# Second chunk's queries loaded in 128-byte pieces and turned on VectorE, and another order of the first stages

## The chip, the cores and the metric

The kernel runs on one core of one Trainium2 chip. The metric is the time of one execution on the device in microseconds; before the change the median of three runs is 737.36 us (735.57 to 737.45).

## The reference

Pooled attention is followed by a gated feed-forward layer. Keys and values are averaged over groups of eight positions (576 become 72), each head's queries attend to the averaged keys, and the result of all heads is the input `x` of 4608 tokens by 512.

```
k_p = k.reshape(B, H, Sp, pool, D).mean(axis=3)          # B = H = 8, S = 576, D = 64, pool = 8
v_p = v.reshape(B, H, Sp, pool, D).mean(axis=3)
scores = scale * np.matmul(q, k_p.transpose(0, 1, 3, 2))
attn = softmax(scores)
x = np.matmul(attn, v_p) as [tokens, heads * D]          # 4608 x 512
a = x @ w1
b = x @ w2
out = (a * b @ w3) @ w_out                               # w1, w2: 512 x 1024; w3: 1024 x 1024; w_out: 1024 x 512
```

## The kernel before

The product `w3 @ w_out` does not depend on the tokens, so it is made first, once, as `W` (1024 x 512); after it each token needs `a`, `b`, their product and one product with `W`. Products run in a 32-bit format with fewer bits, so each operand is split into a high and a low part, and three products (high-high, high-low, low-high) stand for one.

The weights are 64-bit numbers, loaded raw as pairs of 32-bit words and turned into 32-bit numbers on the chip: `w_high` on ScalarE (L144) and `w_low` on VectorE or ScalarE (L149, L154, by the list `LOW_ACT`) make two halves, `w_or` on VectorE (L158) joins them. For `w3` TensorE turns the result (`w_turn`, L187) and `t_hi` (ScalarE, L192) and `t_lo` (VectorE, L195) split it; for `w_out` `o_hi` (L199) and `o_lo` (L203, VectorE or GpSimd by `O_POOL`) do. `w_mm` (L633) multiplies, into the four banks `o0`, `o1`, `o2` and `a` and then `b`; `w_hi` and `w_lo` (L640, L644) split `W`. `w1` and `w2` go the same way without a turn (`load_w12` L135, `w12_high`, `w12_low`, `w12_or`, `w12_hi` L237, `w12_lo` L242 on VectorE or GpSimd by `LO_DVE`). `warm` (L211) is four transposes that nothing reads.

The tokens are worked in 12 chunks of 384. For chunk `m`, `a_mm m j` and `b_mm m j` (L556, twelve products of 128x384 each, j from 0 to 7) fill banks `a` and `b`; `a_post` (L566, ScalarE, or VectorE where `A_DVE` says so) empties `a`, `g_mul` (L574) multiplies, `g_hi` and `g_lo` (L579, L585) split, and `out_mm` (L601) multiplies with `W`. The attention of chunk `n` is done among the products of chunk `n - 1`: keys are averaged by `prep_k` (a tree of three additions on GpSimd, L380 to L385, or a reduction on VectorE, L340, by `K_DVE`), turned by `kt_mm` (L354) and copied by `kt_post`; `s_mm` (L432) makes the scores, `soft_*` on VectorE and ScalarE the softmax, `pt_mm` or `pt_turn` turn it, `av_mm` (L529) multiplies with the averaged values, and `x_hi` and `x_lo` split the result. From the third chunk on one of the score banks is bank `a`.

Queries must be turned before `s_mm`. There are two ways. `load_q3` (L290) loads tokens onto partitions in pieces of 256 bytes, `q3_turn` (L299) turns them on TensorE, three transposes for each of the four pairs of heads, and `q3_post` (L305) copies them out on ScalarE or VectorE (`Q_DVE`). `load_q` (L270) loads blocks of 32 tokens by 32 numbers, 128 bytes at a time, so that `tr_q` (L281), one 32x32 block transpose on VectorE for each pair, puts them in place. `Q3N` lists the chunks that go the first way. The second chunk lies in two batches, so `load_q3` issues two DMAs for a pair of heads and `load_q` eight.

Each step is a function that records its instructions, and `ORDER` names all steps up to the fourth chunk in the order in which they are recorded; the rest follows by due times. Every engine, and SyncE's queue of DMAs, runs its instructions in that order, and semaphores hold it where something it needs is not there.

Of the kernel before, what the change touches and what calls it, by code (L numbers as in the profile page):

```python
# [19 lines left out]
def kernel(  # L20
# [790 lines left out]
    for b in range(1, B):  # L811
# [17 lines left out]
        warm 5; warm 6; w_mm 0 2 (1,); load_w3 4; w_mm 0 3 (0,); t_lo 0; w_mm 1 0 (2,); o_hi 3; o_lo 3;
        w_high w3 3; w_mm 0 2 (0,); w_mm 1 1 (2,); load_wo 2; w_low w3 5; w_low w3 3; w_turn 2; t_hi 2;  # L830
        w_or w3 3; w_mm 0 3 (1,); t_lo 2; w_mm 0 1 (0,); w_mm 0 1 (2,); w_high w3 5; w_mm 1 3 (2,);
        w_mm 1 2 (0,); load_wo 7; w_or w3 5; load_wo 5; w_low w3 4; w_high wo 4; w_low wo 4; w_or wo 4;
        w_mm 1 3 (1,); w_high w3 4; w_or w3 4; w_high wo 2; w_low wo 2; w_or wo 2; w_mm 1 1 (0,); w_mm 1 2 (2,);
        load_w3 6; w_mm 0 1 (1,); w_mm 2 1 (0,1,2); w_mm 0 3 (2,); load_w3 8; w_turn 3; t_hi 3; t_lo 3;
        w_low wo 5; w_low wo 7; w_mm 2 3 (0,1,2); load_wo 6; w_mm 0 2 (2,); w_mm 0 0 (2,); warm 10; w_turn 5;
        w_turn 4; o_hi 2; load_w3 7; w_mm 1 1 (1,); o_lo 2; w_high wo 7; t_hi 4; t_lo 4; w_mm 1 3 (0,);
        w_high wo 5; w_mm 3 1 (0,1,2); o_hi 4; w_high w3 6; w_mm 3 3 (0,1,2); w_or wo 5; w_mm 3 0 (0,1,2);
        load_q3 0 0; w_low w3 6; o_hi 5; w_or w3 6; o_lo 4; w_mm 2 0 (0,1,2); load_w3 10; w_low wo 6; o_lo 5;
        w_low w3 8; w_mm 3 2 (0,1,2); w_mm 4 0 (0,1,2); w_mm 4 2 (0,1,2); t_hi 5; w_high wo 6; t_lo 5;
        w_high w3 7; w_or wo 7; w_low w3 7; w_mm 2 2 (0,1,2); load_k 0 0; load_k 0 1; w_turn 6; t_hi 6;  # L840
        w_mm 4 3 (0,1,2); w_high w3 8; load_q3 0 3; w_or w3 7; w_mm 5 1 (0,1,2); w_mm 5 3 (0,1,2); warm 3;
        w_mm 5 0 (0,1,2); o_hi 7; q3_turn 0 0; q3_post 0 0; w_low w3 10; w_or wo 6; load_w3 9; load_k 0 2;
        o_hi 6; w_turn 7; t_hi 7; w_or w3 8; w_mm 4 1 (0,1,2); t_lo 6; w_mm 5 2 (0,1,2); o_lo 7; o_lo 6;
        load_q3 0 2; w_turn 8; w_mm 6 1 (0,1,2); t_lo 7; w_mm 7 1 (0,1,2); prep_k 0 0; w_mm 6 0 (0,1,2);
        load_w3 11; w_hi 0 0; w_lo 0 0; w_mm 7 3 (0,1,2); w_mm 7 2 (0,1,2); w_high w3 10; w_mm 6 3 (0,1,2);
        q3_turn 0 3; q3_post 0 3; load_q3 0 1; prep_k 0 1; w_low w3 9; load_w3 13; t_hi 8; w_high w3 9; t_lo 8;
        w_or w3 10; prep_k 0 2; w_mm 7 0 (0,1,2); w_mm 6 2 (0,1,2); load_v 0 0; prep_v 0 0; kt_mm 0; w_hi 0 2;
        kt_post 0; load_w3 12; w_mm 8 0 (0,1,2); w_turn 10; w_lo 0 2; w_low w3 11; q3_turn 0 2; t_hi 10;
        w_or w3 9; w_hi 0 1; w_mm 8 3 (0,1,2); q3_post 0 2; t_lo 10; w_lo 0 1; w_high w3 11; w_mm 8 1 (0,1,2);
        load_w3 15; q3_turn 0 1; w_or w3 11; w_turn 9; w_mm 10 3 (0,1,2); warm 11; w_turn 11; w_low w3 13;  # L850
        t_hi 9; t_lo 9; w_mm 8 2 (0,1,2); w_mm 9 1 (0,1,2); warm 1; q3_post 0 1; s_mm 0 (0,); soft_max 0 0 0 0;
        t_hi 11; t_lo 11; w_high w3 13; load_w3 14; load_v 0 1; w_low w3 12; w_hi 0 3; w_mm 9 3 (0,1,2);
        w_mm 9 2 (0,1,2); soft_max 0 0 1 0; w_mm 10 0 (0,1,2); w_mm 9 0 (0,1,2); s_mm 0 (1,); w_mm 10 1 (0,1,2);
        w_high w3 12; w_or w3 13; soft_exp 0 0 0; w_low w3 14; prep_v 0 1; load_w12 0 1; w_mm 10 2 (0,1,2);
        w_or w3 12; w_high w3 14; w_or w3 14; w_turn 14; soft_max 0 1 0 0; soft_max 0 1 1 0; soft_sub 0 1 0 0;
        w_mm 11 1 (0,1,2); soft_sub 0 1 1 0; w_lo 0 3; soft_exp 0 0 1; soft2 0 0; t_hi 14; w_turn 12; w_turn 13;
        load_v 0 2; soft_exp 0 1 0; t_hi 12; t_lo 12; w_mm 11 3 (0,1,2); t_hi 13; w_mm 11 0 (0,1,2); t_lo 14;
        pt_mm 0 0 4 6; w_mm 11 2 (0,1,2); soft_exp 0 1 1; soft_sum 0 1 0; soft_sum 0 1 1; w12_high 0 1; t_lo 13;
        load_w12 0 0; w12_high 0 0; pt_mm 0 0 0 4; w_mm 12 3 (0,1,2); pt_post 0 0 4 6; load_w12 1 1; soft2 0 1;
        load_q3 1 0; w_high w3 15; pt_post 0 0 0 4; s_mm 0 (2,); soft_max 0 2 0 0; w_mm 14 0 (0,1,2);  # L860
        load_q3 1 3; w12_low 0 0; w_mm 12 0 (0,1,2); soft_max 0 2 1 0; pt_mm 0 1 4 6; w12_low 0 1; w12_or 0 0;
        pt_post 0 1 4 6; soft_exp 0 2 0; w12_low 1 1; soft_exp 0 2 1; w_mm 14 1 (0,1,2); w_low w3 15;
        w_or w3 15; pt_mm 0 1 0 4; w_mm 13 3 (0,1,2); w12_high 1 1; w12_or 0 1; w_mm 13 1 (0,1,2); w_turn 15;
        prep_v 0 2; w_mm 14 3 (0,1,2); w_mm 14 2 (0,1,2); w12_hi 0 0; w12_or 1 1; soft2 0 2; load_w12 2 0;
        w12_hi 1 1; q3_turn 1 0; w_mm 12 1 (0,1,2); pt_mm 0 2 4 6; pt_post 0 1 0 4; load_q3 1 1; t_hi 15;
        t_lo 15; w12_low 2 0; w12_lo 0 0; move_v 0 0; load_w12 1 0; w12_low 1 0; w12_high 1 0; w12_or 1 0;
        load_w12 2 1; w12_hi 0 1; w_hi 1 0; pt_mm 0 2 0 4; pt_post 0 2 4 6; pt_post 0 2 0 4; q3_turn 1 1;
        w_mm 15 3 (0,1,2); q3_post 1 0; w_mm 15 1 (0,1,2); q3_post 1 1; w12_low 2 1; w12_lo 1 1; w12_high 2 0;
# [108 lines left out]
```

## Time and profile before

| | |
|---|---|
| runs | 735.57, 737.36, 737.45 us; median 737.36 |
| profiled execution | 736.2 us, its span 734.4 us |
| TensorE busy | 719.3 us (98%) |
| VectorE, ScalarE, GpSimd busy | 404.6, 226.8, 188.2 us |
| mean granted TensorE clock | 0.999 |
| chain that ended last | TensorE 91%, DMA 3%, VectorE 2%, ScalarE 2% |

The span runs from the first to the last instruction of the profiled execution, and 1.8 us of its time lie around it. Busy time of TensorE counts each matmul from its start to its modelled end, and since matmuls overlap, a share of 98% doesn't say that nothing is lost. What is lost is read from its waits and from how far apart its instructions start.

### The profile page before, as it was taken

The numbers are of one execution on the slowest core, as the hardware profiler recorded it, in microseconds if no ns is written. First come the engines' busy times: TensorE is split into PE (matmuls) and PEld (weight loads), VectorE is DVE, ScalarE is ACT, GpSimd is POOL, SyncE is SP. The second block draws the span as 40 slices with busy tenths as digits, with TensorE's granted clock in tenths as the row PEclk, the third lists the DMA queues.
The fourth block names the chain that finished last, engine by engine and source line by source line (L and its number), as shares of the span: only waits on it lengthen the run. The fifth ranks groups of instructions, "written<-read, shape, count | busy, mean of one in ns | idle before, by whom it ended". The sixth has DMA issues, their size and how long they took to land.

```text
span 734.4 us, 13643 instructions
## 1 busy us (share of the span) xinstructions
PE 719.3 (98%) x5450; PEld 650.3 (89%) x5450; DVE 404.6 (55%) x789; ACT 226.8 (31%) x503; POOL 188.2 (26%) x243
## 2 busy tenths in 40 slices
...
GB/s 335 302 252 270 268 165 105 106 109 84 70 58 17 143 65 2 81 127 83 75 113 93 95 65 3 91 124 73 98 100 91 89 65 2 86 24 1 43 1 44
DMA packets 117391, 73.78 MB, mean 100 GB/s; under 512 B 76496, under 2 KB 94416, under 8 KB 117328
## 3 DMA queue, kind: packets, MB, share of 16 engines
...
q10 hardware_dynamic: 144, 0.13, 0.1%
...
## 4 chain that ended last, share of the span: by engine, by line
PE 91%; DMA 3%; DVE 2%; ACT 2%; SPq 1%; issue 1%; POOL 0%; DVEq 0%
PE a L556 27%; PE b L556 27%; PE o L601 26%; PE o L633 3%; PE a L529 3%; PE att L432 2%; DMA st<-in_k_dram 1%; PE a L432 1%; PE b L633 1%; DMA raw<-in_moe_w_dram 1%; PE att L529 1%; PE att L187 1%; DMA PT<-T 1%; PE att L354 0%; DVE EB L449 0%
## 5 line engine op out<-in xcount | busy, mean ns | idle before, releaser
L556 PE MATMUL a<-xT,hl 128*128 128x384 f32 x1152 | 217.4, 336 | 0.2 <-ACT a L566 0.2
L556 PE MATMUL b<-xT,hl 128*128 128x384 f32 x1152 | 216.7, 336 | 0.3 <-DVE a L574 0.3
L556 PEld LDWEIGHTS a<-xT,hl 128*128 128x128 f32 x1152 | 203.4, 188 | 7.7 <-ACT a L566 1.0
L556 PEld LDWEIGHTS b<-xT,hl 128*128 128x128 f32 x1152 | 200.9, 188 | 2.1 <-DVE a L574 0.6
L601 PE MATMUL o<-Wc,gh 128*128 128x512 f32 (+1 forms) x576 | 180.3, 394 | 0.0
L574 DVE TENSOR_TENSOR a<-b,a 128x384 f32<-128x384 f32 x96 | 52.9, 551 | 195.4 <-PE b L556 192.9
L380 POOL TENSOR_TENSOR st<-st 96x512 f32<-96x512 f32 (+3 forms) x52 | 69.5, 1336 | 294.1 <-DMA st<-in_k_dram 207.0
L601 PEld LDWEIGHTS o<-Wc,gh 128*128 128x128 f32 x576 | 105.9, 188 | 22.6 <-issue 4.7
L601 PE MATMUL o<-Wc,gl 128*128 128x512 f32 (+1 forms) x288 | 113.3, 393 | 0.0
L579 ACT CAST gh<-a 128x384 fp32r<-128x384 f32 x96 | 49.3, 513 | 189.7 <-DVE a L574 188.4
L566 ACT COPY a<-a 128x384 f32<-128x384 f32 x91 | 43.6, 479 | 172.7 <-PE a L556 157.0
L585 DVE TENSOR_TENSOR gl<-a,gh 128x384 fp32r<-128x384 f32 x96 | 58.7, 611 | 32.1 <-ACT gh L579 32.1
L601 PEld LDWEIGHTS o<-Wc,gl 128*128 128x128 f32 x288 | 54.1, 188 | 12.5 <-DVE gl L585 0.3
L457 ACT ACTIVATE EB<-EB 128x288 f32<-128x288 f32 x66 | 29.0, 444 | 88.5 <-DVE EB L449 88.5
L508 DVE STREAM_TRANSPOSE T<-EB 128x768 f32<-128x768 f32 x33 | 51.4, 1558 | 6.3 <-DMA PT<-T 6.1
L469 DVE TENSOR_REDUCE sm<-EB 128x4 f32<-128x288 f32 x66 | 29.5, 449 | 28.7 <-ACT EB L457 28.7
L633 PE MATMUL o<-hl 128*128 128x512 f32 x144 | 42.1, 421 | 0.0
L381 POOL TENSOR_TENSOR st<-st 96x256 f32<-96x256 f32 (+3 forms) x52 | 39.8, 766 | 4.1
L398 POOL DMA_DIRECT2D vm<-vp x64 | 32.2, 511 | 2.1 <-POOL vp L385 2.0
L633 PEld LDWEIGHTS o<-hl 128*128 128x128 f32 x144 | 26.7, 197 | 5.9 <-ACT hl L192 0.7
L444 DVE TENSOR_REDUCE mx<-att 128x4 f32<-128x288 f32 (+2 forms) x72 | 28.0, 397 | 3.9 <-PE att L432 3.8
L476 DVE TENSOR_TENSOR EB<-EB,sm 128x576 f32<-128x576 f32 x36 | 28.6, 793 | 1.2
...
## 6 DMA issues: line engine op xcount, KB each, us to landing
...
```

The costliest lines, as they stand in the source:

```text
L380: nc.gpsimd.tensor_tensor(out=t[:, :, 0:4], in0=t[:, :, 0:4], in1=t[:, :, 4:8], op=ALU.add)
L381: nc.gpsimd.tensor_tensor(out=t[:, :, 0:2], in0=t[:, :, 0:2], in1=t[:, :, 2:4], op=ALU.add)
L398: nc.gpsimd.dma_start(out=vm[b % 2][32 * g:32 * g + KW, c], in_=vp[b][KW * i:KW * i + KW, s])
L469: nc.vector.tensor_reduce(out=Mt[n, t][1][:, hs], in_=parts(Et[n, t])[:, hs], axis=AX.XY, op=ALU.add)
L508: nc.vector.transpose(out=T.rearrange("p g u i -> p u g i"), in_=Et[n, t][:, :NU * P].rearrange("p (u j g) -> p u g j", u=NU, g=4))
L556: nc.tensor.matmul(out=o, lhsT=w12[j - j % 2 + kt // 2, w][sw][:, c:c + P], rhs=x[sx][:, kt], start=(i == 0), stop=(i == 3 * NK - 1))
L566: (nc.vector.tensor_copy if (m, j) in A_DVE else nc.scalar.copy)(out=a, in_=stage.pop(("a", m, j))[:, :CH])
L574: nc.vector.tensor_tensor(out=g, in0=ps[:, :CH], in1=g, op=ALU.mult)
L579: nc.scalar.copy(out=gh, in_=g)
L585: nc.vector.tensor_tensor(out=gl, in0=g, in1=f(gh), op=ALU.subtract)
L601: nc.tensor.matmul(out=oacc[m][t][x][:, cols], lhsT=(gh, gl)[sg][:, c], rhs=W[j][sw][:, cols], start=(k == 1 and i == 0), stop=(k == NJ an ...
L633: nc.tensor.matmul(out=wacc[h][it], lhsT=w3t[s][sa][:, x * P:(x + 1) * P], rhs=wo[j][sb], start=n == 1, stop=n == 3 * NJ)
```

## The change

The second chunk is taken out of `Q3N`, so its queries come by `load_q` and are turned by `tr_q`: 12 transposes on TensorE and four copies go, 32 DMAs of 24 KB stand for eight of 96 KB, and VectorE gets four block transposes. Lists that choose an engine change with it: all `a_post` go to ScalarE, some steps of the weights change engine, and the first batch's keys go from VectorE to GpSimd. `ORDER` is another one up to the fourth chunk; after that the steps follow as before.

```
-    LO_DVE = [(0, 0), (1, 0), (1, 1), (2, 0), (7, 0), (7, 1)]
+    LO_DVE = [(1, 1), (2, 0), (2, 1), (3, 1), (4, 0), (4, 1), (6, 0), (6, 1), (7, 1)]
...
-        ('w3', 0), ('w3', 1), ('w3', 10), ('w3', 11), ('w3', 2), ('w3', 3), ('w3', 9), ('wo', 0),
-        ('wo', 4), ('wo', 6)]
-    LOW_DVE = [(0, 1), (1, 1), (2, 1), (5, 0), (7, 1)]
-    O_POOL = [2, 4, 6]
-    A_DVE = [(0, 0), (0, 1), (0, 2), (0, 5), (0, 6)]
-    Q_DVE = [(0, 2), (0, 3), (1, 0), (1, 1), (1, 3)]
-    PT_DVE = [(0, 1, 0), (0, 1, 4), (0, 2, 4), (1, 0, 4), (1, 1, 4), (1, 2, 4)]
+        ('w3', 0), ('w3', 10), ('w3', 13), ('w3', 14), ('w3', 15), ('w3', 2), ('w3', 4), ('w3', 9),
+        ('wo', 2), ('wo', 3), ('wo', 4), ('wo', 7)]
+    LOW_DVE = [(1, 0), (1, 1), (2, 1), (3, 1), (5, 1), (6, 1)]
+    O_POOL = [0, 4, 7]
+    A_DVE = []
+    Q_DVE = [(0, 3)]
+    PT_DVE = [(0, 0, 4), (0, 1, 0), (0, 1, 4), (1, 0, 4), (1, 1, 4), (1, 2, 4)]
     COLD = [0, 1, 10, 11, 2, 3, 4, 6, 7, 8, 9]
-    Q3N = (0, 1)
+    Q3N = (0,)
     PTN = (0,)
-    K_DVE = [(0, 0), (1, 2), (1, 3)]
+    K_DVE = [(1, 3)]
...
-        warm 4; load_wo 0; warm 8; w_high wo 0; warm 7; load_w3 1; w_high w3 1; w_low w3 1; w_low wo 0;
+        load_w3 0; w_low w3 0; w_high w3 0; load_w3 1; w_high w3 1; w_low w3 1; w_or w3 1; w_or w3 0; warm 5;
...
-        a_post 2 5; move_v 2 1; move_v 2 0; av_mm 3; b_mm 2 5; g_hi 2 4; x_hi 3 0; x_hi 3 3; a_mm 2 6; g_lo 2 4;
-        x_lo 3 0; x_lo 3 3; tr_q 4 1; x_hi 3 2; x_lo 3 2; x_hi 3 1; tr_q 4 2; s_mm 4 (0,1,2); g_mul 2 5;
+        a_mm 2 6; x_lo 3 1; b_mm 2 5; g_mul 2 5; s_mm 4 (0,1,2); soft_max 4 1 0 0; soft_sub 4 1 0 0;
```

The first four loads were `wo 0`, `w3 1`, `w3 0`, `w3 2` and are now `w3 0`, `w3 1`, `wo 0`, `w3 2`. Behind `s_mm 4` the two orders differ too: before, `out_mm 2 3`, `out_mm 2 4` and `b_mm 2 6` stand between it and `a_mm 2 7`, which fills bank `a` again; now `out_mm 2 4` alone does. Of the numbers of `warm` only 5 does something.

The first place is TensorE's start. `att<-ident,Wc` are the turns of `w3`, `o<-hl` and `a<-hl` the first products of the weights, and `att<-ident` is `warm`. Before:

```order
L187 MATMUL att<-ident,Wc 128x128 x8
L633 MATMUL o_136<-hl 128x512
L633 MATMUL a<-hl 128x512
L633 MATMUL o_134<-hl 128x512 x2
L633 MATMUL o_136<-hl 128x512
L211 MATMUL att<-ident 128x128 x4
L633 MATMUL o_135<-hl 128x512 x2
```

On the same engine, after the change:

```order
L211 MATMUL att<-ident 128x128 x4
L187 MATMUL att<-ident,Wc 128x128 x8
L633 MATMUL o_154<-hl 128x512
L633 MATMUL a<-hl 128x512
L187 MATMUL att<-ident,Wc 128x128 x4
L633 MATMUL o_154<-hl 128x512
L633 MATMUL o_156<-hl 128x512 x2
```

The warming transposes moved ahead of everything, and a third turn stands after two products.

The second place is ScalarE's start, which makes the first operands: L144 and L154 make the halves of the weights (`Wc` for `w3`, `wt` for `w_out`), L192 is `t_hi`, L199 `o_hi`. Before:

```order
L144 ACTIVATE wt<-raw 128x512
L144 ACTIVATE Wc<-raw 128x512
L154 ACTIVATE Wc<-raw 128x512
L154 ACTIVATE wt<-raw 128x512
L154 ACTIVATE Wc<-raw 128x512
L144 ACTIVATE Wc<-raw 128x512
L199 CAST hl<-wt 128x512
L192 CAST hl<-att 128x512
```

On ScalarE after the change:

```order
L154 ACTIVATE Wc<-raw 128x512
L144 ACTIVATE Wc<-raw 128x512 x2
L144 ACTIVATE wt<-raw 128x512
L144 ACTIVATE Wc<-raw 128x512
L154 ACTIVATE Wc<-raw 128x512
L192 CAST hl<-att 128x512
L199 CAST hl<-wt 128x512
L192 CAST hl<-att 128x512
```

Six operations on weights, the last two on the fourth load (`w3 2`), now stand ahead of the first two splits, where before six stood there too, on three loads.

The third place is SyncE's queue around the second chunk's queries (`qs`); `raw` are loads of `w1` and `w2` there, `st` those of keys and values. Before, from two loads of `w1` and `w2` on:

```order
L135 DMA raw<-in_moe_w_dram 128x2x512 x2
L290 DMA qs<-in_q_dram 64x6x64 x4
L135 DMA raw<-in_moe_w_dram 128x2x512
L290 DMA qs<-in_q_dram 64x6x64 x2
L135 DMA raw<-in_moe_w_dram 128x2x512 x3
L326 DMA st<-in_k_dram 64x512
L326 DMA st<-in_k_dram 128x2x512 x2
L290 DMA qs<-in_q_dram 64x6x64 x2
L135 DMA raw<-in_moe_w_dram 128x2x512 x3
```

On SyncE after the change:

```order
L135 DMA raw<-in_moe_w_dram 128x2x512 x2
L326 DMA st<-in_k_dram 128x2x512
L270 DMA qs<-in_q_dram 32x6x32 x8
L135 DMA raw<-in_moe_w_dram 128x2x512 x3
L270 DMA qs<-in_q_dram 32x6x32 x8
L326 DMA st<-in_k_dram 128x2x512
L135 DMA raw<-in_moe_w_dram 128x2x512
L270 DMA qs<-in_q_dram 32x6x32 x8
L135 DMA raw<-in_moe_w_dram 128x2x512
L326 DMA st<-in_k_dram 64x512
L270 DMA qs<-in_q_dram 32x6x32 x8
```

The loads of queries come in four groups of eight, between loads of weights and keys, where one group of four and two of two stood.

On GpSimd the trees of the first batch's keys were those of the second and third part; now it makes all three, first, third and second, and `kt_mm 0` on TensorE, which needs them, stands behind 105 products of the weights instead of 96.

## Rows read from the trace of the kernel before

**Rows 1.** busy time, share and instructions of each engine, page part 1

```profile
PE 719.3 (98%) x5450; PEld 650.3 (89%) x5450; DVE 404.6 (55%) x789; ACT 226.8 (31%) x503; POOL 188.2 (26%) x243
```

**Rows 2.** TensorE's waits: line and releaser, total us, times, longest

```profile
PE att L187 <- DVE Wc L158: 9.1, 2, 8.6
PE att L354 <- POOL km L385: 0.8, 1, 0.8
PE a L432 <- ACT a L566: 0.6, 1, 0.6
PE b L556 <- DVE a L574: 0.3, 1, 0.3
```

**Rows 3.** TensorE's timeline, first 25 us: start, us, instructions, idle before

```profile
8.64 1.09 PE L187 MATMUL att<-ident,Wc 128*128 128x128 f32 x4 [8.64 <-DVE Wc L158]
...
11.00 0.78 PE L633 MATMUL o<-hl 128*128 128x512 f32 x1
...
13.57 1.06 PE L211 MATMUL att<-ident 128*128 128x128 f32 x4
14.28 2.42 PE L633 MATMUL o<-hl 128*128 128x512 f32 x5
...
18.81 1.30 PE L633 MATMUL o<-hl 128*128 128x512 f32 x5
19.95 0.60 PE L187 MATMUL att<-ident,Wc 128*128 128x128 f32 x4
```

**Rows 4.** windows: busy us by engine (PE, PEld, DVE, ACT, POOL), PEclk, DMA share, GB/s

```profile
10.00:20.00 10.00, 9.77 (x36) 7.60 (x37) 8.90 (x17) 8.37 (x16) 0.00 (x0) 1.00 1.04 404
50.00:60.00 10.00, 10.00 (x111) 7.93 (x109) 9.61 (x22) 7.81 (x25) 6.11 (x8) 1.00 0.99 261
```

**Rows 5.** TensorE's timeline around the second chunk's query transposes, 66 to 78 us

```profile
66.11 0.49 PE L299 MATMUL att<-ident,qs 128*128 128x128 f32 x3
66.35 0.94 PE L633 MATMUL b<-hl 128*128 128x512 f32 x3
67.13 0.38 PE L492 MATMUL a<-ident,EB 128*128 128x128 f32 x2
...
77.37 0.82 PE L299 MATMUL att<-ident,qs 128*128 128x128 f32 x6
77.94 1.30 PE L556 MATMUL b<-xT,hl 128*128 128x384 f32 x6
```

**Rows 6.** groups by shape: line, engine, busy us, mean ns, idle before

```profile
L281 DVE STREAM_TRANSPOSE qT<-qs 128x384 f32<-128x384 f32 x40 | 21.8, 562 | 1.8 <-DMA qs<-in_q_dram 1.8
...
L305 DVE COPY qT<-att 128x384 f32<-128x384 f32 x5 | 3.2, 671 | 1.9 <-PE att L299 1.9
...
L566 DVE COPY a<-a 128x384 f32<-128x384 f32 x5 | 2.7, 549 | 1.1 <-PE a L556 1.1
```

**Rows 7.** SyncE's timeline, query loads: start, us, line, count

```profile
78.33 9.38 SPq L270 DMA_DIRECT2D qs<-in_q_dram  x8
87.76 0.47 SPq L135 DMA_DIRECT2D raw<-in_moe_w_dram  x1
...
89.29 2.77 SPq L270 DMA_DIRECT2D qs<-in_q_dram  x4
```

**Rows 8.** all engines' waits, ScalarE for a weight load: total, times, longest

```profile
ACT wb L144 <- DMA raw<-in_moe_w_dram: 0.7, 1, 0.7
```

**Rows 9.** TensorE's timeline at s_mm 4

```profile
222.49 2.24 PE L556 MATMUL a<-xT,hl 128*128 128x384 f32 x12
225.30 0.27 PE L432 MATMUL a<-kbd,qT 64*64 64x72 f32 x1 [0.57 <-ACT a L566]
```

**Rows 10.** ScalarE's timeline at the start

```profile
6.56 0.66 ACT L144 ACTIVATE Wc<-raw 128x512 f32<-128x512 f32 x1 [1.55 <-DMA raw<-in_moe_w_dram]
7.12 0.64 ACT L154 ACTIVATE Wc<-raw 128x512 int32<-128x512 uint16 x1
7.67 0.66 ACT L154 ACTIVATE wt<-raw 128x512 int32<-128x512 uint16 x1
```

More of the change, by code (lines that the diff above doesn't have):

```diff
@@ L829 @@
[L829 to L868, printed above, removed]
@@ new lines @@
+        prep_v 1 1; w_lo 1 1; a_mm 0 2; w12_high 4 0; w12_or 4 0; load_v 1 2; load_q 2 (0,); load_q 2 (1,);
+        w_lo 1 2; w12_low 5 1; soft_sum 1 0 0; soft_exp 1 0 1; soft_sum 1 0 1; w12_high 4 1; w12_low 4 1;
+        s_mm 1 (1,); w12_or 4 1; w12_high 5 1; prep_v 1 2; g_hi 0 1; b_mm 0 2; w12_hi 4 0; w12_low 5 0;
+        soft2 1 0; load_w12 6 0; soft_max 1 1 0 0; w12_high 5 0; a_post 0 2; soft_exp 1 1 0; g_mul 0 2;
+        w12_or 5 0; g_hi 0 2; out_mm 0 0; soft_max 1 1 1 0; g_lo 0 2; w12_hi 4 1; pt_turn 1 0; a_mm 0 3;
@@ new lines @@
+        s_mm 1 (2,); out_mm 0 2; a_post 0 3; w12_or 5 1; w12_hi 5 0; w12_lo 5 0; load_w12 6 1; w12_hi 5 1;
+        load_w12 7 1; soft_max 1 2 0 0; soft_max 1 2 1 0; g_lo 0 1; w12_low 6 0; b_mm 0 3; soft_sub 1 2 1 0;
+        soft_exp 1 2 1; out_mm 0 1; w12_lo 4 1; w12_lo 4 0; load_w12 7 0; a_mm 0 4; soft_sub 1 2 0 0;
+        soft_exp 1 2 0; soft_sum 1 2 0; pt_move 1 0; g_mul 0 3; w12_high 6 0; soft_sum 1 2 1; soft2 1 2;
+        soft_exp 1 1 1; w12_or 6 0; g_hi 0 3; g_lo 0 3; w12_lo 5 1; load_q 2 (2,); a_post 0 4; move_v 1 0;
@@ new lines @@
+        out_mm 0 4; g_hi 0 5; av_mm 1; x_hi 1 0; x_lo 1 0; x_hi 1 2; x_hi 1 3; b_mm 0 6; g_lo 0 5; x_lo 1 3;
+        a_mm 0 7; g_mul 0 6; g_hi 0 6; g_lo 0 6; load_k 2 2; x_hi 1 1; b_mm 0 7; x_lo 1 1; x_lo 1 2;
+        s_mm 2 (0,1,2); soft_max 2 0 0 0; a_post 0 7; soft_sub 2 0 0 0; soft_max 2 2 0 0; load_k 2 1;
+        out_mm 0 6; soft_exp 2 0 0; g_mul 0 7; soft_max 2 0 1 0; soft_sub 2 0 1 0; soft_exp 2 0 1; prep_k 2 0;
+        prep_k 2 2; out_mm 0 5; soft_max 2 1 0 0; soft_sub 2 1 0 0; g_hi 0 7; a_mm 1 0; a_post 1 0;
@@ new lines @@
+        g_hi 1 1; a_post 1 2; g_lo 1 1; b_mm 1 2; g_mul 1 2; g_hi 1 2; out_mm 1 0; a_mm 1 3; soft_sub 2 2 0 0;
+        soft_exp 2 2 0; b_mm 1 3; soft_sum 2 1 1; a_post 1 3; soft_exp 2 2 1; load_q 3 (1,); tr_q 3 1;
+        out_mm 1 1; a_mm 1 4; g_lo 1 2; out_mm 1 2; kt_mm 2; soft_sum 2 2 0; b_mm 1 4; soft2 2 1; pt_turn 2 1;
+        pt_move 2 1; tr_q 3 3; a_mm 1 5; a_post 1 4; soft_sum 2 2 1; g_mul 1 3; load_k 3 0; b_mm 1 6; soft2 2 2;
+        prep_k 3 0; load_v 2 1; g_hi 1 3; pt_turn 2 2; g_lo 1 3; pt_move 2 2; av_mm 2; tr_q 3 2; a_post 1 5;
```

157 lines of the change are left out of this document (88 added, 69 removed).

## Prediction

> **What bounds the kernel now.** I read the shares of busy time first: TensorE is busy 719.3 of the 734.4 us of the profiled execution, VectorE 404.6, ScalarE and GpSimd far less [rows 1]. So the end is set by how much TensorE has to do and by the few places where it stands still. The second view is TensorE's waits, and there the reader sees how little is to be had: 9.1 us for the first weights, nearly all of it before its first instruction, then 0.8 us for `km` from GpSimd, 0.6 us for `a` from ScalarE, and one of 0.3 us [rows 2]. The third view is TensorE's timeline at the start. It begins at 8.64 us with the first transposes and at 11.00 us with the first product, and it is slow there: five products of 128x512 span 2.42 us at 14.28 us, and 1.30 us at 18.81 us [rows 3]. The granted clock of that stretch is given as 1.00 throughout [rows 4], so the durations have to tell it: the earlier five ran at the lower of the two levels (1.2 GHz), the later five at the upper (2.4 GHz), after TensorE had transposed and multiplied with short gaps since 8.64 us. A microsecond at the lower level loses 1 - 1.30/2.42 = 0.46 us of work. From the first products on, all gains and losses are sums of a few tenths, against 0.3% of the time, 2.2 us, which is about what a measurement of this kernel can tell from no change.
>
> **The change part by part.**
>
> *The transposes of the second chunk's queries* leave TensorE: four `q3_turn`, of three transposes each. A group of three starts at 66.11 us and the product behind it at 66.35, so 0.24 us; the two groups that stand together start at 77.37 and the next product at 77.94, so 0.57 us [rows 5]. The fourth group reads like the first. That is 0.24 + 0.24 + 0.57 = 1.05 us. The products behind such a group are slower too: three of them take from 66.35 to 67.13, 0.78 us [rows 5], where five in a row take from 18.81 to 19.95, which is 0.23 each [rows 3], so 0.69 for three. With 0.09 us at each of three places the sum is **-1.3 us**; the bounds are -1.05 and -1.4. It lies wholly on the path, since TensorE is the path.
>
> *What comes in their place* lies on other engines. VectorE gets four `tr_q`, 0.56 us each, 2.2 us. It loses four copies of turned queries (0.67 us each, three of the second chunk and one of the first: 2.7 us) and the five `a_post` of the first chunk (0.55 us each: 2.7 us) [rows 6], so it comes out some 3 us lighter in a stretch where it is busy 9.61 of 10 us [rows 4]. That is cover: VectorE's part I cost at nothing, and if the cover were gone it would cost at most the 2.2 us of the four transposes. ScalarE takes the five `a_post` over and has room (7.81 of 10 us) [rows 4].
>
> *SyncE* issues 32 loads of 24 KB in place of eight of 96 KB. In the trace eight loads of this kind, those of a later chunk with twice the bytes each, held the queue for 9.38 us from 78.33 us on [rows 7]. Behind the new loads stand the loads of `w1` and `w2`, and behind these the splitting of the weights for the first `a_mm` and `b_mm`. One such load was already waited for by ScalarE, 0.7 us [rows 8]. I cost it at nothing, because the new loads go out in four groups of eight with half the bytes each and a weight load in between, and keep the other end for the rival below.
>
> *The wait on GpSimd before `kt_mm 0`* [rows 2]. In the new order this group of transposes stands behind 105 matmuls of the weight product, not 96. GpSimd adds the tree over the first keys, which VectorE did before, but it does nothing at all from 10 to 20 us [rows 4], and its last tree is now that of the keys that were its first. Nine more products at 0.23 us give 2.1 us of cover for a wait of 0.8, so I take **-0.8 us**. The other end: if loads hold the third tree back, the wait stays, so 0.
>
> *The wait before `s_mm 4`* [rows 9]. Twelve `a` products end, and the first score product waits 0.57 us for ScalarE to empty bank `a`. The new order puts `b_mm 2 5`, twelve more products, between the two: 225.30 - 0.57 - 222.49 = 2.2 us of TensorE's time. That covers the copy: **-0.6 us**, and the other end is 0. What is late next: `a_mm 2 7` needs the same bank again, and there is now one `out_mm` between `s_mm 4` and it where two and a `b_mm` stood, so VectorE's minima and differences of bank `a` have less time. That is the wait that the change adds; queued behind it on TensorE is everything.
>
> *The head.* The order of the first loads changes: `w3 0`, `w3 1`, `wo 0`, `w3 2`. The second load lands before 6.56 us, when ScalarE's wait for it ends [rows 10]; at 404 GB/s [rows 4] each further 512 KB takes 1.3 us, so the fourth lands at 6.56 + 2 x 1.3 = 9.2 us. ScalarE then has, in this order, the high and the low half of `w3 2`, `t_hi 1`, `o_hi 0` and `t_hi 0`. It starts one such operation every 0.55 us (7.12 to 7.67), and one takes 0.64 [rows 10]: 9.2 + 4 x 0.55 + 0.64 = 12.0 us. The first product needs both `o_hi 0` and `t_hi 0`, so it starts at 12.0, not at 11.00: +1.0 us. Against this the four warming transposes, which hold TensorE from 13.57 to 14.28 us [rows 3], now stand before everything, in time that is idle anyhow: -0.7 us. Together **+0.3 us**, if the clock rises when it does now. Each microsecond earlier or later is 0.46 us, and two either way is what I allow: -0.6 to +1.2.
>
> *Other new waits.* The order is new over some 230 us, and the old one left two waits there, of 0.8 and 0.6 us. I expect about half of one: **+0.4 us**, between 0 and 1.5.
>
> The sum: -1.3 - 0.8 - 0.6 + 0.3 + 0.4 = **-2.0 us**. The profiled execution took 736.2 us (its span is 734.4, the rest lies around it), so it would take 734.2. The three runs shown have the median 737.36, and 735.57 is the lowest; their mean is 736.8. I apply the sum to that mean, since the profiled run stands between them too, and forecast **734.8 us**.
>
> **The rivals.** *The new loads hold the weights back.* This is the one on the slower side. When a large backlog is in front, eight loads in 128-byte pieces hold SyncE for 9.38 us, where the weight load behind them is issued in 0.47 [rows 7]; eight times that is 3.8, so 5.6 us are lost. The first new group goes out behind two weight loads and a key load, much as those at 78.33 did. It decides once the weights of `a_mm 0 0` to `a_mm 0 3` come later than ScalarE's turn for them, and the 0.7 us wait [rows 8] says that some have nothing to spare. With 1 us of cover: 734.8 + 4.6 = 739.4. Against it: the new loads have half the bytes each, and the four loads from 89.29 us, with three larger ones just ahead, took 2.77 us, 0.69 each [rows 7], so the hold is not the rule. The Trainium skill ("DMA: Bandwidth & Descriptors", Specifications) names 512 bytes as the least transfer for full rate and says that below it the engine reads, modifies and writes; pieces of 128 bytes are under that. By that rule alone this rival would be the outcome, 739.4 us. The trace bears it out in part: in 50 to 60 us, with 256-byte pieces among the loads, the DMA engines are busy 0.99 and move 261 GB/s, against 404 at 1.04 with large ones [rows 4].
>
> *The clock and the new waits eat it.* The first products come 1.0 us later, and behind a hole, since the first transposes need only the second load. If the level rises 2 us later, that is +0.9 us, and one whole new wait of 0.8 in place of half: 734.8 + 0.9 + 0.4 = 736.1 us, or 737 with one more. For it: the level rose only after sustained work now [rows 3]. Against it: nothing in the trace shows what the hole would do.
>
> *More than the sum.* The clock rises 2 us earlier (-0.9), no new wait comes (-0.4), and the wait of 0.3 us for VectorE's `a` [rows 2] is gone: 734.8 - 0.9 - 0.4 - 0.3 = 733.2 us.
>
> *VectorE does not do the turning in time.* The change then costs a wait for `qT` at `s_mm 1`; but three microseconds less work on VectorE speak against it, and it would be some tenths. I count it with the second rival.
>
> **How the numbers follow.** My forecast, -2 us with 1 us either way, has 0.50; more than the sum 0.10; clock and waits 0.26; the loads 0.14. Faster by over 0.3% of 737.36 means below 735.15: 0.43 of the forecast's 0.50 and the 0.10, so 0.53. Within 0.3%: the rest of the forecast and the second rival, 0.33. Slower: 0.14. The range leaves out half of the third case's 0.10 below and most of the slow one above: 732.6 to 739.0.
>
> **What would show it.** In the profile after: no transposes on the line of `q3_turn` after the first chunk, and 12 fewer matmuls; among TensorE's waits no `km` of 0.8 and no `a` before `s_mm 4`; the first product near 12.0 us, and the place where five 128x512 products fall from 2.4 to 1.3 us no later than 17 us. Wrong would be: TensorE waiting for `hl` of `w1` or `w2` between 75 and 110 us with SyncE's query issues over 1 us each (the loads), a product at the lower level beyond 18 us (the clock), or a wait of over 1 us that no place above names.

## The result, and the profile after

The changed kernel takes 739.91 us (median of five runs, 739.4 to 740.92) where the kernel before, run beside it, took 735.78 us (735.0 to 737.45). The ratio is 1.0053, with a 95% interval of 1.0037 to 1.0069: it is slower, by some 4 us, and 739.91 us lies above the range of the prediction. The profiled execution of the changed kernel took 740.92 us with a span of 739.1 us, 4.7 us more than that of before.

The shares first, as page part 1 has them (busy time, share and instructions of each engine):

```profile
PE 720.2 (97%) x5438; PEld 649.3 (88%) x5438; DVE 401.9 (54%) x782; ACT 228.9 (31%) x509; POOL 189.8 (26%) x246
```

TensorE has as much to do as before [rows 1], 12 matmuls fewer, and a span that is 4.7 us longer. So it stands still more. Its waits (line and releaser, total us, times, longest):

```profile
PE att L187 <- DVE Wc L158: 5.6, 1, 5.6
PE a L492 <- DVE PT L502: 2.1, 1, 2.1
PE o L633 <- ACT hl L192: 2.0, 1, 2.0
PE att L211 <- POOL ident masks.py:199: 1.4, 1, 1.4
PE o L601 <- DVE gl L585: 1.2, 1, 1.2
PE a L492 <- DVE EB L476: 1.2, 1, 1.2
PE a L556 <- ACT a L566: 0.9, 1, 0.9
```

The waits on `km` and before `s_mm 4` [rows 2] are gone, as forecast. In their place stand 2.1 and 1.2 us on L492, where TensorE turns the first chunk's probabilities, 1.2 us on L601 and 0.9 us on L556. The head of TensorE's timeline (start, us, instructions, idle before):

```profile
1.36 1.12 PE L211 MATMUL att<-ident 128*128 128x128 f32 x4 [1.36 <-POOL ident masks.py:199]
8.09 1.97 PE L187 MATMUL att<-ident,Wc 128*128 128x128 f32 x8 [5.61 <-DVE Wc L158]
12.03 0.80 PE L633 MATMUL o<-hl 128*128 128x512 f32 x1 [1.97 <-ACT hl L192]
...
16.03 2.61 PE L633 MATMUL o<-hl 128*128 128x512 f32 x7
...
18.71 1.08 PE L633 MATMUL o<-hl 128*128 128x512 f32 x4
```

The first product starts at 12.03 us, where the working had 12.0. The clock rises within the seven products from 16.03 us on, which take 0.37 us each on the mean, between the 0.48 of five at the lower level and the 0.26 at the upper [rows 3]; the four from 18.71 us on are at the upper one.

Where the 4.7 us come from shows when the same products are set side by side. The starts, in us, are read from the three traces (the last column is the experiment with few loads, below):

| | before | after | after minus before | few loads minus before |
|---|---|---|---|---|
| first product of the weights | 11.00 | 12.03 | +1.0 | +1.0 |
| 49th | 27.00 | 27.50 | +0.5 | +0.1 |
| 157th | 62.82 | 61.90 | -0.9 | -1.4 |
| 192nd, the last | 75.03 | 77.82 | +2.8 | -1.4 |
| 241st product with `w1` or `w2` | 142.20 | 148.62 | +6.4 | +0.5 |
| 577th (behind `s_mm 4`) | 239.78 | 245.73 | +5.95 | 0.0 |
| 1969th | 636.86 | 642.65 | +5.8 | -0.1 |
| 2017th | 650.48 | 655.21 | +4.7 | -1.2 |

Until 62 us the change is ahead by 0.9 us. Between 62 and 78 us it loses 3.7, and between there and 149 us 3.6 more, of which the kernel with few loads loses 1.9 too. Behind that it gains some 0.5 us around `s_mm 4`, and another 1.05 around 640 us, where the orders are the same.

What TensorE waited for on L492 was VectorE, and VectorE's timeline shows what that waited for (start, us, instructions, idle before and its releaser):

```profile
64.18 0.43 DVE L149 TENSOR_SCALAR wb<-raw 128x512 int32<-128x512 int32 x1 [1.57 <-DMA raw<-in_moe_w_dram]
...
68.62 0.43 DVE L149 TENSOR_SCALAR wb<-raw 128x512 int32<-128x512 int32 x1 [1.72 <-DMA raw<-in_moe_w_dram]
68.96 0.42 DVE L502 COPY PT<-a 128x256 f32<-128x256 f32 x1
```

The low halves of two loads of `w1` and `w2` (L149) wait for their loads, 1.57 and 1.72 us. The normalising of the first chunk's softmax (L473 to L476) and the copy of turned probabilities (L502) stand behind them on VectorE, and TensorE can't turn on without these. SyncE's timeline shows why the loads are late (start, us, line, count):

```profile
52.71 7.07 SPq L270 DMA_DIRECT2D qs<-in_q_dram  x8
59.88 1.45 SPq L135 DMA_DIRECT2D raw<-in_moe_w_dram  x3
61.38 7.54 SPq L270 DMA_DIRECT2D qs<-in_q_dram  x8
...
69.93 0.40 SPq L135 DMA_DIRECT2D raw<-in_moe_w_dram  x1
70.39 4.69 SPq L270 DMA_DIRECT2D qs<-in_q_dram  x8
...
76.23 4.29 SPq L270 DMA_DIRECT2D qs<-in_q_dram  x8
```

The four groups of eight query loads hold the queue for 7.07, 7.54, 4.69 and 4.29 us, 23.6 us in all. The eight loads of before held it for 2.67 + 1.27 + 1.29 = 5.2 us in its timeline:

```profile
52.90 2.67 SPq L290 DMA_DIRECT2D qs<-in_q_dram  x4
...
58.78 1.27 SPq L290 DMA_DIRECT2D qs<-in_q_dram  x2
...
69.48 1.29 SPq L290 DMA_DIRECT2D qs<-in_q_dram  x2
```

The three weight loads of the changed kernel at 59.88 us stand behind the first group, and the next one, at 69.93, behind the second.

### The profile page after: what moved, and what is told of

Same layout as the page of the kernel before. It is cut to its first block, busy times and chain, and to the rows that moved or that the text cites. A ratio compares the mean times of both kernels' runs of the same rounds, so it can differ in the third digit from the quotient of the medians.

```text
span 739.1 us, 13659 instructions
## 1 busy us (share of the span) xinstructions
PE 720.2 (97%) x5438; PEld 649.3 (88%) x5438; DVE 401.9 (54%) x782; ACT 228.9 (31%) x509; POOL 189.8 (26%) x246
## 4 chain that ended last, share of the span: by engine, by line
PE 86%; DMA 7%; DVE 3%; POOL 1%; SPq 1%; ACT 1%; issue 0%; DVEq 0%
PE o L601 26%; PE b L556 25%; PE a L556 25%; DMA raw<-in_moe_w_dram 4%; PE a L529 3%; PE o L633 2%; PE att L432 1%; DMA qs<-in_q_dram 1%; DMA st<-in_v_dram 1%; PE a L432 1%; DMA PT<-T 1%; DVE T L508 1%; PE att L529 1%; POOL st L380 1%; DVE hl L242 0%; PE a L633 0%
## 5 line engine op out<-in xcount | busy, mean ns | idle before, releaser
L556 PE MATMUL a<-xT,hl 128*128 128x384 f32 x1152 | 217.7, 336 | 0.9 <-ACT a L566 0.9
L556 PE MATMUL b<-xT,hl 128*128 128x384 f32 x1152 | 216.9, 335 | 0.1
L556 PEld LDWEIGHTS a<-xT,hl 128*128 128x128 f32 x1152 | 203.3, 188 | 9.0 <-ACT a L566 1.3
L556 PEld LDWEIGHTS b<-xT,hl 128*128 128x128 f32 x1152 | 200.8, 188 | 1.7 <-DVE hl L242 0.4
L601 PE MATMUL o<-Wc,gh 128*128 128x512 f32 (+1 forms) x576 | 180.4, 394 | 0.0
L601 PEld LDWEIGHTS o<-Wc,gh 128*128 128x128 f32 x576 | 105.8, 188 | 23.0 <-issue 5.0
L601 PE MATMUL o<-Wc,gl 128*128 128x512 f32 (+1 forms) x288 | 113.3, 393 | 1.2 <-DVE gl L585 1.2
L566 ACT COPY a<-a 128x384 f32<-128x384 f32 x96 | 46.1, 480 | 182.9 <-PE a L556 162.6
L601 PEld LDWEIGHTS o<-Wc,gl 128*128 128x128 f32 x288 | 54.1, 188 | 13.9 <-DVE gl L585 1.6
L381 POOL TENSOR_TENSOR st<-st 96x256 f32<-96x256 f32 (+3 forms) x54 | 43.2, 799 | 4.2
L476 DVE TENSOR_TENSOR EB<-EB,sm 128x576 f32<-128x576 f32 x36 | 28.9, 803 | 1.4
```

Of the source, the lines that this page charges most:

```text
L381: nc.gpsimd.tensor_tensor(out=t[:, :, 0:2], in0=t[:, :, 0:2], in1=t[:, :, 2:4], op=ALU.add)
L556: nc.tensor.matmul(out=o, lhsT=w12[j - j % 2 + kt // 2, w][sw][:, c:c + P], rhs=x[sx][:, kt], start=(i == 0), stop=(i == 3 * NK - 1))
L566: (nc.vector.tensor_copy if (m, j) in A_DVE else nc.scalar.copy)(out=a, in_=stage.pop(("a", m, j))[:, :CH])
L601: nc.tensor.matmul(out=oacc[m][t][x][:, cols], lhsT=(gh, gl)[sg][:, c], rhs=W[j][sw][:, cols], start=(k == 1 and i == 0), stop=(k == NJ an ...
```

## The experiments

After the comparison of the traces three theories were left. **Number**: the queue's time goes by how many loads there are, since each has to be issued, and a load may have to wait until an earlier one has landed. **Pieces**: 128-byte pieces are slow to move. **Order**: the new order makes VectorE late, whatever the loads do.

All medians below stand beside runs of the kernel before on the same chip (736.35, 736.15 and 736.13 us in the three sets). The ratios are to those; that of the changed kernel is to its own 735.78.

| kernel | loads of the second chunk's queries | median us | ratio | 95% interval |
|---|---|---|---|---|
| after | 32 of 24 KB, 128-byte pieces | 739.91 | 1.0053 | 1.0037 to 1.0069 |
| x1_old_way | 8 of 96 KB, 256-byte pieces, turned on TensorE | 737.34 | 1.0013 | 0.9999 to 1.0028 |
| x11_old_way_late | the same, three turns later | 736.36 | 1.0005 | 0.9993 to 1.0017 |
| x2_long_pieces | 32 of 24 KB, 768-byte pieces | 738.19 | 1.0026 | 1.0008 to 1.0043 |
| x3_few_short | 8 of 96 KB, 128-byte pieces | 734.04 | 0.9970 | 0.9957 to 0.9983 |
| x6_few_short | the same again | 734.07 | 0.9972 | 0.9958 to 0.9987 |
| x9_number | the same, and 24 of 2 KB | 738.94 | 1.0041 | 1.0027 to 1.0055 |
| x7_vec_order | as after, VectorE's two waiting steps later | 740.18 | 1.0052 | 1.0029 to 1.0074 |
| x8_spread | as after, spread | 741.93 | 1.0088 | 1.0072 to 1.0104 |
| x10_early | as after, 12 ahead of the first `w1` load | 739.22 | 1.0044 | 1.0028 to 1.0060 |
| x5_pool | as after, issued by GpSimd | 748.49 | 1.0173 | 1.0155 to 1.0191 |
| x4_before_tr | before's order, 32 of 24 KB | 741.96 | 1.0075 | 1.0052 to 1.0099 |
| x12_before_two | before, two waits taken away | 739.31 | 1.0044 | 1.0028 to 1.0061 |

### The old loads in the new order

```
-    Q3N = (0,)
+    Q3N = (0, 1)
...
-        load_q 1 (0,); ... tr_q 1 0;
+        load_q3 1 0; ... q3_turn 1 0; q3_post 1 0;
```

> The changed kernel with the second chunk's queries loaded and turned in the old way (eight loads in 256-byte pieces, 12 transposes on TensorE, four copies), at the places of the new loads; the rest is the new order. Three theories. Number: a load on SyncE's queue cannot go out before the load eight places ahead of it has landed, so 24 more loads hold the queue and the weights come late. Pieces: 128-byte pieces are slow to move and hold the queue. Order: the new order itself makes VectorE late, whatever the loads. By the number and by the pieces the waits of TensorE at 65 us (1.2), 69 us (2.1), 97 us (0.9) and 121 us (1.2) go and 1.3 us of transposes come back: 739.9 - 5.4 + 1.3 = 735.8 us. By the order they stay: 741.2 us.

It took 737.34 us. The waits on L492 fell from 3.3 to 0.8 us, but the turns, all placed in one stretch just ahead of the first chunk's products, waited themselves (0.8 and 0.6 us). With three of the four turns behind `a_mm 0 0`:

> The new order with the second chunk's queries loaded and turned in the old way, three of the four turns placed behind the first products of the first chunk. The kernel with all of them ahead of these products took 737.3 us and showed waits of 0.8, 0.8 and 0.6 us at or just ahead of the turns. If these belong to the place of the turns, 735.2 to 736 us; if the order itself makes them, 737 to 738 us.

736.36 us. So the new order with the old loads is as fast as the kernel before, and the 4 us come with the loads, not with the order.

### The number and the pieces, one at a time

The same 32 loads, each of them reading one 768-byte piece per partition:

```
+                        if n == 1:
+                            h = s0 + db * (cnt // 2)
+                            src = q[b, 2 * pr + par, h:h + cnt // 2, :].rearrange(
+                                "(t u) e -> t (u e)", t=32)
```

> The changed kernel with the 32 loads of the second chunk's queries kept in number, size and place, but each read from DRAM in one 768-byte piece per partition in place of six of 128 bytes (the queries of that chunk then are not the right ones, so the result of that chunk is not computed). Number: the queue still waits for the load eight places ahead, so 739 to 740 us. Pieces: the waits go, 734.5 to 736 us. Order: 739.9 us.

And eight loads of 96 KB that keep the 128-byte pieces, their number and the bytes, each over 128 partitions in place of 32 and from other rows of the queries, some of them read twice:

```
+                        if n == 1:
+                            if g == 0:
+                                nc.sync.dma_start(
+                                    out=t[:, pr, off // 32:(off + cnt) // 32],
+                                    in_=q[b, pr % 2:pr % 2 + 6, s0:s0 + P, 0:32].rearrange(
+                                        "h t e -> t h e"))
+                            continue
```

> The changed kernel with eight loads of 96 KB in place of 32 of 24 KB, at the same places, still in 128-byte pieces, the same bytes and as many pieces (read from other rows of the queries, so the result of that chunk is not computed). Number: the queue is free as it was before the change, 734.5 to 736 us. Pieces: the time stays, 739 to 740 us. Order: 739.9 us.

> The kernel with eight loads of 96 KB in 128-byte pieces once more (the second chunk's queries come from other rows, so the result of that chunk is not computed), since its profiled execution was a disturbed one: 734 us, no wait of TensorE over 0.5 us between 60 and 130 us, and SyncE's issues of these loads 0.6 to 1 us each with no held gaps.

Long pieces took 738.19 us and few loads 734.04 and 734.07. From the ratios, and each time from the changed kernel on, the number is worth 1.0053 - 0.9972 = 0.8% or 6 us, and the pieces 1.0053 - 1.0026 = 0.3% or 2 us, with an uncertainty of about 1.7 us on either. With few loads TensorE's waits are these, of which all but the one on L608 (L601 of the changed kernel) lie ahead of the first products:

```profile
PE att L187 <- DVE Wc L158: 5.6, 1, 5.6
PE o L640 <- ACT hl L192: 1.9, 1, 1.9
PE o L608 <- DVE gl L592: 1.5, 1, 1.5
PE att L211 <- POOL ident masks.py:199: 1.4, 1, 1.4
```

and the DMA engines are busy where they stood partly idle in the changed kernel. Windows of the changed kernel (busy us of PE, PEld, DVE, ACT and POOL, PEclk, DMA share, GB/s):

```profile
50.00:60.00 10.00, 10.00 (x109) 7.91 (x107) 8.82 (x18) 8.96 (x25) 4.97 (x8) 1.00 0.63 187
60.00:70.00 10.00, 6.71 (x45) 5.19 (x38) 5.66 (x15) 5.30 (x21) 4.20 (x7) 1.00 0.63 189
```

and of the kernel with few loads:

```profile
50.00:60.00 10.00, 10.00 (x112) 7.98 (x110) 9.41 (x19) 8.63 (x23) 6.36 (x10) 1.00 0.93 285
60.00:70.00 10.00, 10.00 (x81) 7.87 (x86) 8.33 (x19) 9.33 (x29) 6.17 (x8) 1.00 1.03 297
```

0.63 against 0.93 and 1.03. So in the changed kernel the pieces are not what the DMA engines are full of; they stand partly idle while SyncE's queue is held. With few loads the queue has room: from 50 to 82 us it waits 12.4 us for TensorE to free a place for weights (`SPq L135 <- PE o L640`), against 6.0 in the changed kernel. That is 6.4 us of room, and 32 loads ask for 23.6 - 4.6 = 19 us more.

The cleanest test adds the number alone: the eight loads, and behind each of them three loads of 2 KB, in pieces of 64 bytes, into a tile that nothing reads.

```
+                            if g:
+                                nc.sync.dma_start(
+                                    out=stage["tiny"][:, 6 * pr + (3 if off else 0) + g - 1],
+                                    in_=q[b, 2 * pr, s0 + 32 * g:s0 + 32 * g + 32, 0:16])
```

> The kernel with eight loads of 96 KB (734.05 us; the second chunk's queries come from other rows, so that chunk's result is not computed) and, behind each of them, three loads of 2 KB into a tile that nothing reads. So there are 32 loads again at the same places, with 48 KB and 768 pieces more than with eight. If the number of loads is what costs, 738 to 740 us with the queue's waits on earlier loads back; if it is bytes or pieces, 734 to 734.5 us.

738.94 us: 24 loads with 48 KB among them cost 4.9 us. The wait on L492 is back (here L505), and in SyncE's own waits from 50 to 82 us the new loads (L274) wait for earlier ones:

```profile
PE a L505 <- DVE PT L515: 1.9, 1, 1.9
```

```profile
SPq L274 <- DMA raw<-in_moe_w_dram: 3.8, 5, 2.2
SPq L274 <- DMA st<-in_k_dram: 1.3, 2, 1.1
```

TensorE's clock isn't the cause: it fell in the profiled execution of this kernel, but the four of its eight executions with a mean granted clock of 1.00 took 738.56 to 739.41 us.

The groups hold the queue for 22.7 us in its timeline, little less than the 23.6 with 24 KB loads and the 22.4 with long pieces, and five times the 4.6 us with eight loads. What they do in that time shows in the same view of the changed kernel:

```profile
SPq L270 <- DMA raw<-in_moe_w_dram: 6.1, 5, 2.5
...
SPq L270 <- DMA st<-in_k_dram: 1.1, 1, 1.1
```

Of the 23.6 us, 6.1 + 1.1 = 7.2 are query loads that wait for an earlier load to land, of the weights above all. In the trace each load of this queue waits for, and then raises, one of eight semaphores in turn, so that a load can't go out before the one eight places ahead has landed; a load of 2 KB takes a place as one of 512 KB does. The other 16.4 us are the issues themselves, 0.51 us each. In the kernel before no query load waits for another load in that stretch. The Trainium skill ("DMA: Bandwidth & Descriptors", Anatomy of one DMA, on loads that GpSimd issues) says that DMA engines do not wait on semaphores and that such a wait happens on the issuing sequencer. Here the loads are SyncE's, and it is its queue that stands still for those 7.2 us, so the trace agrees.

The Trainium skill ("DMA: Bandwidth & Descriptors", Specifications) names 512 bytes as the least transfer for full rate. The prediction weighed the pieces by that rule. Here it does not carry the cost: pieces of 768 bytes, above that limit, gave back about 2 us of the changed kernel's time, and fewer loads with pieces of 128 bytes about 6.

### Which step passes the delay on

On VectorE, the two waiting steps moved behind the work that TensorE needs first:

```
-        w12_low 1 0; soft2 0 1; ... w12_low 1 1; load_w12 2 0; pt_post 0 1 4 6; w12_or 1 0;
+        soft2 0 1; ... pt_post 0 1 4 6; w12_low 1 0; w12_low 1 1; load_w12 2 0; w12_or 1 0;
```

> The changed kernel with two steps moved on VectorE: the low halves of the weights of load 1 0 and load 1 1, which wait for their loads, now stand behind the normalising of the first chunk's second and third part and behind a copy of turned probabilities, not ahead of them. If TensorE's waits at 65 us (1.2) and 69 us (2.1) come from what is queued behind these two waits on VectorE, they go: 739.9 - 3.3 = 736.6 us, and with some of it given back where the weights are used, 737 to 738. If VectorE is late for another reason, 739.5 to 740.5 us.

Both waits on L492 are gone, and in the profiled execution the last weight product starts at 73.96 us in place of 77.82. Some of that is lost again where TensorE waits before L556, 0.9 us in the changed kernel:

```profile
PE a L556 <- ACT a L566: 1.6, 1, 1.6
```

The wait on L601 stays as it was, 1.2 us. This execution took 738.09 us, 2.8 less than the profiled one of the changed kernel. But the median of the seven is 740.18 us (737.04 to 741.54), no less than the changed kernel's, and no trace shows where the slower ones lose it. So the queue on VectorE passes the delay on, which the two waits show that went. What the other order of VectorE is worth by itself is not settled.

### Other places and another queue

Spread two or three at a time behind each load of weights or keys (`load_w12 1 0; lq 0 3 6;` and so on, where `lq` issues a part of one pair's eight):

> The changed kernel with the 32 loads of the second chunk's queries spread, two or three behind each weight or key load from 52 us on, in place of four groups of eight. By the number, the load eight places ahead is then seldom one of a group that has only just gone out and two weight loads are under way at any time, so the weights come earlier: 735 to 738 us. If it is the sum of the issues that holds the queue, however they are placed, the time stays at 739 to 740 us.

741.93 us, slower still. Two loads of weights go out at 54.81 and 59.02 us, where the changed kernel has three from 59.88 us on. But the queries come later, and VectorE, which takes things in order, waits for those:

```profile
63.68 0.58 DVE L285 STREAM_TRANSPOSE qT<-qs 128x384 f32<-128x384 f32 x1 [2.47 <-DMA qs<-in_q_dram]
...
71.39 0.58 DVE L285 STREAM_TRANSPOSE qT<-qs 128x384 f32<-128x384 f32 x1 [1.46 <-DMA qs<-in_q_dram]
...
83.25 0.58 DVE L285 STREAM_TRANSPOSE qT<-qs 128x384 f32<-128x384 f32 x1 [3.11 <-DMA qs<-in_q_dram]
```

TensorE then waits for VectorE ahead of the second chunk's scores (`s_mm 1`, here L436):

```profile
PE att L436 <- DVE qT L285: 2.7, 1, 2.7
```

By its timeline the query loads hold the queue for 17.3 us in place of 23.6. They wait 1.3 us for earlier loads in place of 7.2, and loads of weights and keys wait 2.8; the issues take 16.0 us against 16.4. So fewer waits for a place brought no time back here; spreading chose who is late.

Twelve of the loads moved ahead to where the queue was idle:

> The changed kernel with 12 of the 32 loads of the second chunk's queries moved ahead, to where SyncE's queue stands idle behind the last load of w3 (44 to 50 us), and the others moved up, so that 20 in place of 32 stand between the loads of w1 and w2. If the weights are late because of the loads queued ahead of them, about a third of the 5.9 us between 32 loads and eight comes back: 737 to 738 us; if the early loads only push the last w3 loads or the first w1 loads back, 739.5 to 741 us.

739.22 us. The twelve hold the queue for 9.8 us, 3.2 of them in waits for earlier loads of weights, and the first load of `w1` goes out at 53.19 us in place of 50.17:

```profile
43.28 9.81 SPq L274 DMA_DIRECT2D qs<-in_q_dram  x12
53.19 0.90 SPq L135 DMA_DIRECT2D raw<-in_moe_w_dram  x2
```

ScalarE waits for that load with the last halves of `w3` behind it, VectorE waits for these, and TensorE for a split that stands behind them on VectorE:

```profile
57.92 0.66 ACT L144 ACTIVATE wb<-raw 128x512 f32<-128x512 f32 x1 [4.31 <-DMA raw<-in_moe_w_dram]
```

```profile
PE att L436 <- DVE hl L195: 3.3, 1, 3.3
```

The median hides two groups. Four of the ten executions, the profiled one among them, had a mean granted clock of 0.998 to 1.00 and took 737.62 to 737.86 us; the six others, at 0.994 to 0.997, took 739.21 to 742.00. So where the clock held, about the expected third of the 6 us came back, and where it fell, it was lost again.

All 32 through GpSimd's queue:

```
-                        nc.sync.dma_start(
+                        (nc.gpsimd if n == 1 else nc.sync).dma_start(
```

> The changed kernel with the 32 loads of the second chunk's queries issued by GpSimd's queue in place of SyncE's; number, pieces, bytes and place in the order stay. If what costs is that the weight loads stand behind these loads in SyncE's queue, the weights come in time and the time is near that of the kernel with eight loads: 734 to 736 us, and over it as far as GpSimd, which has to issue them among its own work, makes others wait. If what costs is the moving of the pieces by the DMA engines, it stays at 739 to 740 us.

748.49 us. The waits on L492 are gone here too, but GpSimd issues in its own time, and its splitting of weights (`w12_lo`, L242) stands behind its issues:

```profile
PE a L556 <- POOL hl L242: 4.3, 1, 4.3
PE att L432 <- DVE qT L281: 4.2, 1, 4.2
```

With these two waits the granted clock falls, to 0.50 from 80 to 85 us and from 90 to 95, so part of the 748.49 us is the clock and not the queue.

### The loads in the old order

```
-    Q3N = (0, 1)
+    Q3N = (0,)
...
-        load_q3 1 0; ... q3_turn 1 0; ... q3_post 1 0;
+        load_q 1 (0,); ... tr_q 1 0;
```

> The kernel before, in its old order, with one change: the second chunk's queries come by the 32 loads of 24 KB and are turned by VectorE, at the places of the old loads and copies. Number and pieces: the weights come late here too and TensorE gets new waits, 737 to 740 us. Order: nothing but the 12 transposes goes, 735.8 - 1.3 = 734.5 us.

741.96 us, 5.6 more than before. ScalarE's timeline, and the wait of TensorE that it leads to:

```profile
68.19 0.66 ACT L154 ACTIVATE wb<-raw 128x512 int32<-128x512 uint16 x1 [3.72 <-DMA raw<-in_moe_w_dram]
73.15 0.66 ACT L154 ACTIVATE wb<-raw 128x512 int32<-128x512 uint16 x1 [4.30 <-DMA raw<-in_moe_w_dram]
...
75.24 0.60 ACT L502 COPY PT<-att 128x512 f32<-128x512 f32 x1
```

```profile
PE a L529 <- ACT PT L502: 7.9, 1, 7.9
```

Here it is ScalarE that waits for weights, 3.72 and 4.30 us, with the last copies of the probabilities behind it. The mechanism is the same in another order, on another engine. Some of the 5.6 us is the clock: it is granted at 0.71 from 70 to 75 us and at 0.61 from 75 to 80.

### The two waits taken away in the kernel before

`kt_mm 0` placed behind `w_mm 8 0`, and `out_mm 2 3` ahead of `s_mm 4`:

> The kernel before with the two waits of TensorE taken away that my sum counted on, and nothing else: kt_mm 0 stands behind three more products of the weights, and out_mm 2 3 stands ahead of s_mm 4. If the two terms are right, 0.8 + 0.6 = 1.4 us less than before; if the waits only move to the next place, no difference.

739.31 us, slower by 3.2. Both waits are gone. But `s_mm 4` now starts at 227.16 us in place of 225.30, VectorE's softmax follows as much later, and behind that on VectorE stands the `g_lo` for which `out_mm 2 5` now waits. TensorE's timeline there:

```profile
237.80 0.68 PE L601 MATMUL o<-Wc,gl 128*128 128x512 f32 x1 [1.96 <-DVE gl L585]
238.27 1.05 PE L601 MATMUL o<-Wc,gh 128*128 128x512 f32 x2
239.13 0.63 PE L601 MATMUL o<-Wc,gl 128*128 128x512 f32 x1
```

TensorE stands still for 1.96 us, and then two products of 128x512 start 0.86 us before the third (238.27 to 239.13) where two of those at the upper level take 0.46 us [rows 3]. The granted clock is 0.80 on the mean from 235 to 240 us, so part of that stretch is at 1.2 GHz:

```profile
235.00:240.00 5.00, 3.04 (x11) 2.13 (x10) 3.73 (x5) 0.92 (x2) 0.00 (x0) 0.80 0.18 41
```

What was gained at `kt_mm 0` also went again: the 157th weight product is 0.8 us earlier than before (0.3 of it stood already at the 49th), the 181st 0.2 later.

## Why the prediction was wrong

- **The step that failed is the one on SyncE**, "I cost it at nothing". The loads cost about 6 us. The working argued from half the bytes per load, and from an issue of 0.69 us where no backlog stands in front. But the queue's time went by the number of loads: 0.51 us for each issue, and 7.2 us of waiting for earlier loads to land, which the kernel before does not show there. 32 loads in place of eight should have been priced as 24 more issues at 0.5 us, 12 us of the queue, in a stretch where the DMA engines are busy 0.99 before the change [rows 4].
- **The rival on the slower side was the outcome**: its place (weight loads behind query loads) was right and its time, 739.4 us, is 0.5 from the measured one. That the two times agree so well is luck. The rival stood 2.6 us above the mean of 736.8 that it was added to; the measured time is 4.1 above 735.78. And its price was reached by another way than it came about. It took the cost to be the hold by short pieces behind a backlog; x2, x6 and x9 put most of it down to the number. It also looked for the damage at `a_mm 0 0` to `a_mm 0 3`, and by the table 4.2 of the 5.9 us against the kernel with few loads came earlier, by way of VectorE's order. Its sign did not show either: TensorE waits for no `hl` between 75 and 110 us, and the 32 issues take 0.44 us in the median, one of them over 1. The chance of 0.14 was too low: it should have been asked what a queue does with four times as many loads, whatever their size.
- **VectorE "some 3 us lighter"** was true (401.9 against 404.6 us busy [rows 1]) and worth nothing, since VectorE was late for want of loads, not of time.
- **The wait before `kt_mm 0` and that before `s_mm 4`** are gone, as the working said. The second is seen in the table (some 0.5 us between 149 and 246 us). The first is part of the 0.9 us that the change is ahead at the 157th product. x12 shows that neither is a gain by itself: what was behind the wait comes earlier and meets the next late operand.
- **The head** came out about as worked out: first product at 12.03 us, and 0.5 us lost by the 49th product where +0.3 was forecast. The clock did not rise "when it does now", though: by the starts of the products, 0.43 us apart at the lower level and 0.23 at the upper, it rose at about 17.7 us, where the sign had 17 at the latest and the kernel before about 16.4. In other kernels with the same head the 49th product starts between 26.4 and 27.5 us, with the clock rising sooner or later, and with the old head (before, x4, x12) between 25.8 and 27.0, so the allowance of -0.6 to +1.2 was about right.
- **"Other new waits", +0.4 us**, was too small. Before L601 the wait behind `g_lo` shows in every kernel with the new order, from 0.3 us in x1 and x11 to 1.5 in x6, where the loads are not in the way. Some 1.05 us come back around 640 us, which no term had: in the profiled executions of before and of x12 TensorE has lost that much there, in those of x4 and of the new orders it has not. VectorE waits there 2.34 us for a DMA of turned probabilities in before and 0.39 us in x4, with the same order. Why is open.
- **The transposes** are gone (12 matmuls fewer). Nearest to a measurement of them is x11 against x6, which differ in the transposes with their copies, the block transposes in their place and the loads' pieces: 1.0005 - 0.9972 = 0.33% or 2.4 us, with an uncertainty of 1.4, where the term had 1.3. The whole of the sum but the loads is x6: 0.9972 of 736 us is 2.1 us less, between 1.0 and 3.1, where the sum had 2.0. By the table, that agreement is of totals: the -1.4 us up to the 157th product, +1.9 behind it, -0.5 around `s_mm 4` and -1.05 around 640 us are not the terms that were added up.

What stays open: how much of the 6 us goes to the issues and how much to waiting for a place. They came together in all runs but x8, where the waits fell and the queries came late instead. And no version was found that computes everything and beats the kernel before. x6 would, but it reads other rows of the queries.
